# A gated mix of sliding-window attention and a SwiGLU block on one core: projections moved forward, one half-tile later, last operands scaled before the product

## The chip, the cores and the metric

The kernel runs on one core of one Trainium2 chip. The metric is the time of one execution on the device, in microseconds (us); lower is better. The core has five engines that run side by side and wait for one another through semaphores: TensorE (PE in the profile; its weight loads are PEld), VectorE (DVE), ScalarE (ACT), GpSimd (POOL) and SyncE (SP), whose queue issues most of the transfers.

## The reference

Two branches work on the same input `x` (2048 rows of 512) and are mixed row by row by a gate:

```python
def _A_ref(x, wqkv, wo):                       # attention
    B, S, D = x.shape
    H = 32; Dh = D // H; W = 256
    ... q, k, v of (x @ wqkv), 32 heads of 16
    scores = q @ k.T * Dh ** -0.5
    mask = (i - j >= 0) & (i - j < W)          # causal, the last 256 positions
    p = softmax(where(mask, scores, -1e9))
    return (p @ v) @ wo

def _B_ref(x, w_gate, w_up, w_down):           # F = 1792
    return (silu(x @ w_gate) * (x @ w_up)) @ w_down

g = sigmoid((x * gate_w).sum(-1, keepdims=True))
return g * _A_ref(...) + (1 - g) * _B_ref(...)
```

## The kernel before, in words

All products are formed from 32-bit operands split in two: a value is rounded to a high part (a cast on ScalarE), the rest is the low part (a subtraction on GpSimd or VectorE), and three matmuls (high by high, high by low, low by high) stand for one product. `split` at lines 64 to 70 does that; its cast is line 67, its subtraction line 70, whoever calls it.

The schedule is written out by hand: each engine runs its instructions in the order in which the program issues them, and so does each queue of transfers. The 32 heads are worked in 8 groups of 4; a block is 128 rows, a chunk (`c`) 512 rows, of which there are four, and a half (`hf`) two chunks.

**Start.** Nine matmuls on a tile of ones (18 in the trace, line 206) run while the input comes in; GpSimd fills the tile first (line 203), in the memory of a key tile. Then come, each as 12 whole matmuls from line 231 with a bank of PSUM as the target: the query and key projections `proj(g, c)` of groups 0 and 1, and V's blocks 0 to 3. `proj` ends with a copy out of PSUM on ScalarE (line 274) and a split; `stack(g, hf)` then moves a half's rows by twelve transfers on SP's queue (lines 284 and 285) into the tiles `QT` and `KT`, from which scores are formed.

**V's blocks.** V's blocks 4 to 15 follow in pairs on the two halves of the array's rows (`lanes`, line 251), pairs on `pb` and on `pa` by turns. Each pair takes two banks; ScalarE copies them out (line 442) and GpSimd sends them to `vd`. Woven in between are the 64 score matmuls of group 0 (`stage1`, line 301), each followed on VectorE by mask and row maximum (line 303); `put_max` (lines 314 to 319) writes a half's maxima into a row of `QT`. Behind V's blocks come, before the change, `proj(1, 2)`, `proj(1, 3)`, `stack(1, 1)` and the loads of V (`load_v`, line 330).

**Main loop.** 128 steps `t`, each of four sub-steps `hd`; four steps form a quad with the parts 0 to 3. In a sub-step PE does one score matmul of the next group (`stage1`), one transposed score matmul of this group (`stage2`, line 343, followed by the exponential on ScalarE, line 345, and selects on GpSimd, lines 347 and 350), and six lane matmuls of a projection or of the gate and up products (line 251; `unit` hands out four turns a quad: two on `pa`, two on `pb`). Once a quad the product with V is formed (`av`, line 367), and the generator `FIN` finishes the quad before: `finish` has five parts, a ScalarE copy (382), a VectorE addition out of PSUM (384), a transpose (388), reciprocal and multiplication (392, 393), and a transpose with a store (396, 397). Everything else is put into a table by step and sub-step with `later(t, hd, ...)` and runs when the loop gets there. In `group_half`, which takes up the projections of groups 2 to 7, each half has two splits, `half(0)` and `half(1)`, and then its `stack`. In the last 16 steps the scores of a next group are gone, and weights of the down projection are prepared instead (`early`, lines 653 and 657) with the row gate (637).

**The end.** The output projection and the down projection (a scheme of seven products of blocks, in the order of `ITEMS`) run as whole matmuls, three per product (`mm3`, lines 85 to 87); `halve` splits an operand, `JOBS` holds VectorE's work on finished banks, `DO` what is due at an item, and `scaled` multiplies a result by the gate (line 951), adds (953) and sends it (955). The last output tile is formed in two halves of 256 columns from the last three items; behind it VectorE multiplies by the gate (1072), adds the rest (1073) and SP sends it (1074).

Of the kernel before, what the change touches and what calls it, by code (L numbers as in the profile page):

```python
# [8 lines left out]
F32 = mybir.dt.float32  # L9
F32R = mybir.dt.float32r  # L10
AF = mybir.ActivationFunctionType
ALU = mybir.AluOpType
# [3 lines left out]
P = 128  # L16
S, D, H, DH, W, F = 2048, 512, 32, 16, 256, 1792
NK = D // P
NB = S // P
CH = 512  # L20
NCH = S // CH
# [14 lines left out]
def gated_mix(ctx, tc, xT, xn, w1a, w1b, wqk, wv, wo, wgu, wd, gw, outT):  # L36
# [4 lines left out]
    nc = tc.nc  # L41
# [16 lines left out]
    ring = ctx.enter_context(tc.tile_pool(name="ring", bufs=2))  # L58
# [32 lines left out]
    def run(gen, n=None):  # L91

        while n is None or n > 0:
            if next(gen, run) is run:
                break
            n = n and n - 1
# [5 lines left out]
    def slot(name, dtype=F32R):  # L102
        return stk.tile([P, S], dtype, name=name)
# [6 lines left out]
    KT = [[slot(f"k0{pr}") for pr in range(2)]]  # L110
# [82 lines left out]
    pp = ctx.enter_context(tc.tile_pool(name="pp", bufs=2, space=PSUM))  # L193
# [4 lines left out]
    with ExitStack() as A:  # L198
        sm = A.enter_context(tc.tile_pool(name="sm", bufs=2))


        ones = KT[0][0][:, :P].bitcast(F32)
        nc.gpsimd.memset(ones, 1.0)
        warm = pp.tile([P, CH], F32, name="pa")
        for _ in range(9):
            nc.tensor.matmul(warm[:, :P], ones, ones, start=True, stop=True)
# [13 lines left out]
        def x_pair(pool=None, name="x"):  # L220
            return tuple((pool or sm).tile([P, 2 * CH], F32R, name=f"{name}{w}", bufs=1) for w in ("hi", "lo"))
# [44 lines left out]
        def proj(g, c, pool, name):  # L266

            hf, cc = divmod(c, 2)
            if cc == 0:
                X[g, hf] = x_pair() if g == hf else x_pair(vpool, f"x{g}{hf}")  # L270

            def done(ps):
                raw = kept()
                nc.scalar.copy(raw, ps)
                split_qk(g, hf, cc, raw)
            todo = products(("p", g), c)
            return whole(pool, name, swapped(todo) if g == c == 0 else todo, done)

        def stack(g, hf):
            for pr in range(2):  # L280
                q, k = (halves_of(t[g % 2][pr])[hf] for t in (QT, KT))
                hi, lo = (x[32 * pr:] for x in X[g, hf])
                for b, (qx, kx) in enumerate(((hi, hi), (hi, lo), (lo, hi))):
                    nc.sync.dma_start(q[b::4].bitcast(F32), qx[:32].bitcast(F32))
                    nc.sync.dma_start(k[b::4].bitcast(F32), kx[64:96].bitcast(F32))
# [223 lines left out]
            run(proj(0, c, pp, "pa"))  # L509
        stack(0, 1)  # L510
        stack(1, 0)


        first = chain(*(stage1(0, b) for b in range(NB)))
# [12 lines left out]
                put_max(0, 0)  # L527
        run(first)
        put_max(0, 1)
        for c in range(2, NCH):  # L530
            run(proj(1, c, pp, "pb"))
        stack(1, 1)
        for n in range(4):
            load_v(n)
        vp.close()
# [6 lines left out]
        def later(t, hd, *fs):  # L542
            AT.setdefault((t, hd), []).extend(fs)
# [46 lines left out]
        def group_half(t, g, hf):  # L590

            t0 = t + 3 + hf

            def done(ps):
                places = [kept(), kept()]
                for m in range(2):
                    later(t0, 2 * m, lambda m=m: nc.scalar.copy(places[m], ps[m]))

                def half(m):
                    if m == 0:  # L600
                        X[g, hf] = x_pair()
                    split_qk(g, hf, m, places[m])
                first = t0 + (3 + g % 2) * hf
                later(first, 3, lambda: half(0))
                later(first + 1, 1, lambda: half(1))
                later(max(first + 1, (g - 1) * NB) if hf else first + 1, 3, lambda: stack(g, hf))
            return done

# [69 lines left out]
        for b in range(NB):  # L678
            t, hd = blocks[b]
            later(t, hd, lambda b=b: gate_block(b))  # L680
            if b > 1:
                t, hd = blocks[b - 2]
# [13 lines left out]
        FIN = iter(())  # L696
        for t in range(G * NB + 1):
            g, i = divmod(t, NB)
            d, part = divmod(t, NSLOT)
            if part == 0:  # L700
                turns = unit(t) if t < G * NB else [iter(())] * NSLOT
            s1 = stage1(g + 1, i) if t < g7 else iter(())
            s2 = stage2(g, i) if t < G * NB else iter(())
            for hd in range(4):
                run(s1, 1)
                if t < g7:
                    run(s2, 1)
                elif hd % 2 == 0:
                    run(s2, 2)
                run(turns[part], 3)  # L710
                for f in AT.pop((t, hd), ()):
                    f()
                if (part, hd) in ((0, 2), (1, 1), (1, 3), (2, 1)):
                    run(FIN, 1)
                if hd == 1 and part == 0:
                    if t:
                        ag, c = divmod(d - 1, NCH)
                        av(ag, c)
                        FIN = finish(ag, c)
                        run(FIN, 1)  # L720
            if i in (7, 15) and g + 1 < G:
                later(t + 1, 2, lambda g=g, i=i: put_max(g + 1, i // 8))
            if t >= 10 and t % 4 == 2 and t + 6 < G * NB:
                load_v((t + 6) // 4)
# [6 lines left out]
    with ExitStack() as B:  # L731
        got = B.enter_context(tc.tile_pool(name="got", bufs=10, side="right"))
        hp = B.enter_context(tc.tile_pool(name="hp", bufs=LEAD + 2, side="right"))
# [13 lines left out]
        def load_wo(k):  # L747
            raw = taken(wo[:, k])
            return lambda: split(woh[:, k], wol[:, k], raw, nc.scalar, nc.vector)
# [4 lines left out]
        PLACE = {}  # L754
# [30 lines left out]
        ITEMS = [("a", c, k) for c in range(NCH) for k in range(NK)]  # L785
# [4 lines left out]
        SRC, HALF, PARTS = {}, {}, {}  # L790
# [101 lines left out]
        GATE = {}  # L892
# [71 lines left out]
        def after(p, pr):  # L964

            two = bank(p, pr)
            for d in range(2):
                m = 2 * pr + d
                if p == 1:
                    JOBS.append(lambda d=d, m=m: nc.scalar.copy(saved(m), two[d]))  # L970
                if p == 5:
                    JOBS.append(lambda d=d, m=m: nc.scalar.copy(saved(4 + m), two[d]))
                if p == 6:
                    JOBS.append(lambda d=d, m=m: nc.vector.tensor_tensor(out=spare(m), in0=two[d], in1=saved(4 + m), op=ALU.subtract))
                if p == 2:
                    JOBS.append(lambda d=d, m=m: combined(2 * pr, d, two[d], saved(m), ALU.add))
                if p == 7:
                    JOBS.append(lambda d=d, m=m: combined(2 * pr + 1, 2 + d, two[d], saved(4 + m), ALU.subtract))
                if p == 3:
                    JOBS.append(lambda d=d, m=m: combined(2 * pr + 1, d, two[d], spare(m), ALU.add))  # L980
                if p == 4 and pr == 0:
                    JOBS.append(lambda d=d: scaled(2 * pr, 2 + d, column(), two[d]))

        late = [load_wo(k) for k in range(NK)]
        for e in ITEMS[:LEAD]:
            load(e)
# [21 lines left out]
        end = len(ITEMS) - 3  # L1008

        DO = {}  # L1010

        def on(n, f, *args):
            DO.setdefault(n, []).append(lambda: f(*args))

        for j in range(2 * NP):
            two = divmod(j, 2)
            n = WO + j
# [20 lines left out]
        for i in range(NP):  # L1038
            n = WO + 57 + 4 * (i // 2) + i % 2 - (i == 6)
            steps(n, (n + 6, n + 7), negated, NP + i)  # L1040
        for n, e in enumerate(ITEMS[:end]):
            if n + LEAD + AHEAD < WO:
                load(ITEMS[n + LEAD + AHEAD])
            for f in DO.pop(n, ()):
                f()
            while rows and at[(*rows[0], 0)] <= n + 6:
                load_sum(*rows.pop(0))
            if n + LEAD < len(ITEMS):
                halve(ITEMS[n + LEAD])
            if JOBS:  # L1050
                JOBS.pop(0)()
            if e[0] == "a":
                multiply_a(*e[1:])
                continue
            p, k, pr = e
            block(e)
            HALF.pop(e)
            if k == NP - 1:
                after(p, pr)
        while JOBS:  # L1060
            JOBS.pop(0)()
        two, t, part, rest = bank(4, 1), *(column() for _ in range(3))
# [4 lines left out]
        for cols in (slice(0, CH // 2), slice(CH // 2, CH)):  # L1067
            ps = pp.tile([P, CH], F32, name="pa")[:, cols]
            for n, (p, k, pr) in enumerate(ITEMS[end:]):
                hh, hl = HALF[p, k, pr]  # L1070
                mm3(ps, [(block_weights(p, k, 1), (hh[:, cols], hl[:, cols]))], start=n == 0, stop=n == 2)
            nc.vector.tensor_tensor(out=part[:, cols], in0=ps, in1=GATE[1][:, 2, cols], op=ALU.mult)
            nc.vector.tensor_tensor(out=part[:, cols], in0=part[:, cols], in1=rest[:, cols], op=ALU.add)
            nc.sync.dma_start(place(2, 3)[:, cols], part[:, cols])


# [34 lines left out]
```

## Time and profile before

| | |
|---|---|
| median of 3 runs | 801.77 us (801.17 to 802.3) |
| profiled execution | 801.55 us, of which the span from first to last instruction is 799.9 us |
| busy share of the span | PE 99%, PEld 87%, DVE 78%, ACT 54%, POOL 43% |
| mean HBM traffic | 119 GB/s |

Busy time of PE is no measure of speed by itself: matmuls overlap and their ends are modelled. What can be read exactly is the distance between the starts of two matmuls, and how far it is above what the same two take elsewhere in the trace.

### The profile page before, as it was taken

The page shows a single profiled execution, that of the slowest core. Times are in us where ns is not written, and L with a number is a line of the kernel's source. Part 1 is how long each engine was busy: PE and PEld are TensorE (multiplying, and loading weights), DVE is VectorE, ACT ScalarE, POOL GpSimd, SP SyncE. Part 2 cuts the span into 40 slices and gives each one's busy share as a digit, 9 for nine tenths or more (in the row PEclk, how much of TensorE's full clock was granted, in tenths as well). Part 3 has the DMA queues.
Part 4 walks back from the last instruction along what each step waited for, and adds up shares of the span by engine and source line. Part 5 has one row for each costly group of instructions (what it writes and reads, how often), then busy time and mean ns, then how long its engine had stood idle before and what let it go on. Part 6 is the DMA issues. An engine that isn't in the chain of part 4 may idle for free.

```text
span 799.9 us, 21441 instructions
## 1 busy us (share of the span) xinstructions
PE 794.2 (99%) x8247; PEld 698.2 (87%) x8247; DVE 626.2 (78%) x1689; ACT 432.6 (54%) x883; POOL 342.1 (43%) x643
## 2 busy tenths in 40 slices
PE   9999999999999999999999999999999999999998
PEld 8888999889889989899998998888988888888886
DVE  5397787878886887878776888888675478899896
ACT  7422556565565567555666656555643235554642
POOL 6712456565546556544656454546740111000112
PEclk9999999999999999999999999999999999999999
DMA  8574515425242453351533516425537898717435
GB/s 302 168 217 147 142 69 137 131 90 151 68 153 81 114 168 103 112 156 59 145 111 120 152 51 195 144 90 186 190 105 251 285 342 293 288 57 272 93 55 104
DMA packets 62107, 121.88 MB, mean 152 GB/s; under 512 B 10868, under 2 KB 19828, under 8 KB 61748
## 3 DMA queue, kind: packets, MB, share of 16 engines
q1 hardware_dynamic: 54756, 99.01, 40.1%
q0 software_dynamic: 7104, 21.24, 9.0%
q8 instruction: 65, 1.06, 0.6%
q14 instruction: 38, 0.31, 0.1%
q10 hardware_dynamic: 144, 0.26, 0.1%
HBM read 55.97 MB, written 39.34 MB: 119 GB/s over the span
## 4 chain that ended last, share of the span: by engine, by line
PE 98%; DVE 2%; issue 0%; POOL 0%; POOLq 0%
PE pa L251 24%; PE pb L251 24%; PE ps L301 7%; PE ps L343 5%; PE ps L367 5%; PE ps L87 4%; PE ps L86 4%; PE ps L85 4%; PE pb L367 4%; PE pa L231 2%; PE pb L231 2%; PE pa L87 2%; PE pb L86 2%; PE pa L86 2%; PE pb L87 2%; PE pb L85 2%
## 5 line engine op out<-in xcount | busy, mean ns | idle before, releaser
L303 DVE CUSTOM_DVE_ANT_0 ps<-ps,mask 128x384 f32<-128x384 f32 (+2 forms) x512 | 268.5, 540 | 99.4 <-PE ps L343 52.1
L345 ACT ACTIVATE pt<-ps 128x384 f32<-128x384 f32 (+2 forms) x512 | 238.0, 474 | 127.5 <-PE ps L343 68.0
L347 POOL TENSOR_SCALAR_AFFINE_SELECT pt<-pt 128x256 f32<-128x256 f32 x256 | 110.7, 433 | 197.4 <-ACT pt L345 195.5
L343 PE MATMUL ps<-q,k 64*128 64x384 f32 (+2 forms) x512 | 162.3, 335 | 0.0
L301 PE MATMUL ps<-k,q 63*128 63x384 f32 (+2 forms) x512 | 159.6, 332 | 0.5 <-DVE mx L303 0.5
L251 PE MATMUL pb<-xhi,wh 64*128 64x512 f32 x512 | 117.0, 396 | 0.0
L251 PE MATMUL pb<-xlo,wh 64*128 64x512 f32 x512 | 115.7, 391 | 0.0
L251 PE MATMUL pa<-xhi,wh 64*128 64x512 f32 x512 | 115.7, 394 | 0.0
L251 PE MATMUL pb<-xhi,wl 64*128 64x512 f32 x512 | 115.6, 391 | 0.0
L251 PE MATMUL pa<-xlo,wh 64*128 64x512 f32 x512 | 114.4, 392 | 0.0
L251 PE MATMUL pa<-xhi,wl 64*128 64x512 f32 x512 | 114.3, 391 | 0.0
L301 PEld LDWEIGHTS ps<-k,q 63*128 63x128 f32 x512 | 88.9, 185 | 13.4 <-DVE mx L303 3.3
L350 POOL TENSOR_SCALAR_AFFINE_SELECT pt<-pt 128x256 f32<-128x256 f32 x224 | 98.4, 439 | 0.0
L343 PEld LDWEIGHTS ps<-q,k 64*128 64x128 f32 x512 | 91.3, 185 | 5.2 <-issue 0.2
L303 DVE DVE_READ_ACCUMULATOR2_ANT mx<- 128x1 f32 x512 | 71.4, 139 | 0.0
L367 PE MATMUL ps<-pt,vg 64*32 64x320 f32 (+4 forms) x1408 | 70.6, 344 | 0.0
L367 PE MATMUL pb<-pt,vg 64*32 64x256 f32 (+3 forms) x1360 | 69.9, 349 | 0.0
L251 PEld LDWEIGHTS pb<-xhi,wh 64*128 64x128 f32 x512 | 63.1, 186 | 4.1 <-DVE o L384 0.3
L251 PEld LDWEIGHTS pb<-xhi,wl 64*128 64x128 f32 x512 | 62.6, 185 | 3.6
L251 PEld LDWEIGHTS pa<-xhi,wl 64*128 64x128 f32 x512 | 61.3, 185 | 3.9
L251 PEld LDWEIGHTS pb<-xlo,wh 64*128 64x128 f32 x512 | 62.6, 186 | 0.2
L251 PEld LDWEIGHTS pa<-xhi,wh 64*128 64x128 f32 x512 | 60.8, 186 | 1.9
(303 smaller groups left out, 1601.0 us busy)
## 6 DMA issues: line engine op xcount, KB each, us to landing
kept_h<-ev SPq DMA_DIRECT2D x52, 256.0 KB
od<-o POOLq DMA_DIRECT2D x32, 256.0 KB, 3.5
raw<-wgu SPq DMA_DIRECT2D x28, 256.0 KB
q<-xhi SPq DMA_DIRECT2D x56, 128.0 KB
k<-xhi SPq DMA_DIRECT2D x56, 128.0 KB
outT<-sg POOLq DMA_DIRECT2D x28, 256.0 KB, 4.0
vd<-vs POOLq DMA_DIRECT2D x8, 672.0 KB, 4.9
vg<-vd SPq DMA_DIRECT2D x32, 168.0 KB
```

What stands on the lines that cost most here:

```text
L85: nc.tensor.matmul(ps, lh, rh, start=start and i == 0, stop=False, skip_group_check=skip)
L86: nc.tensor.matmul(ps, lh, rl, start=False, stop=False, skip_group_check=skip)
L87: nc.tensor.matmul(ps, ll, rh, start=False, stop=stop and i == n - 1, skip_group_check=skip)
L231: nc.tensor.matmul(ps, w, x, start=n == 0, stop=n == len(todo) - 1)
L251: mm = nc.tensor.matmul(ps[me], w[r], x[r], start=not second and i == 0, stop=bool(second) and i == n - 1)
L301: nc.tensor.matmul(ps[:, :n], QT[g % 2][pr][r, q0:q0 + P], KT[g % 2][pr][r, k0:k0 + n], start=True, stop=True)
L303: mx = nc.vector.tensor_tensor_reduce(out=ps[:, :n], in0=ps[:, :n], in1=mask[:, 3 * P - n:], scale=1.0, scalar=NEG, op0=ALU.add, op1=ALU.m ...
L343: nc.tensor.matmul(ps[:, :n], KT[g % 2][pr][r, k0:k0 + P], QT[g % 2][pr][r, k0:k0 + n], start=True, stop=True)
L345: BEHIND.append(nc.scalar.activation(pt[:, j, :n], ps[:, :n], AF.Exp, scale=SCALE))
L347: nc.gpsimd.affine_select(out=pt[:, :, :P], in_=pt[:, :, :P], pattern=[[0, 2], [1, P]], compare_op=ALU.is_ge, fill=0.0, base=0, channel_mu ...
L350: nc.gpsimd.affine_select(out=pt[:, :, 2 * P:], in_=pt[:, :, 2 * P:], pattern=[[0, 2], [-1, P]], compare_op=ALU.is_ge, fill=0.0, base=-1, ...
L367: nc.tensor.matmul(AV[g, c][h][32 * j:32 * j + 32, q0 - c * CH:q1 - c * CH], VG[4 * g + kb // 4][o, kb % 4, 17 * j:17 * j + 32], PT[g, kb, ...
```

## The change

Four edits in one:

1. The warm-up matmuls read a constant that the program's preamble has filled, instead of a tile that GpSimd fills.
2. `proj(1, 2)`, `proj(1, 3)` and `stack(1, 1)` come ahead of V's blocks 4 to 15, directly behind `stack(1, 0)`; they stay on `pb`.
3. In `group_half`, `half(1)` of the second half (`hf` 1) of odd groups runs at sub-step 3 instead of 1; and in the main loop the parts of `FIN` that fall on a sub-step are issued ahead of what the table holds for it.
4. For the last tile the three operands are multiplied by the gate and split before the product (`SCALED`), issued behind the last item of the main list; behind the product only the addition is left.

```diff
-        ones = KT[0][0][:, :P].bitcast(F32)
-        nc.gpsimd.memset(ones, 1.0)
+        ones = nc.const_aps.tensor(1.0, [P, P], F32)
...
         stack(0, 1)
         stack(1, 0)
+        for c in range(2, NCH):
+            run(proj(1, c, pp, "pb"))
+        stack(1, 1)
...
         run(first)
         put_max(0, 1)
-        for c in range(2, NCH):
-            run(proj(1, c, pp, "pb"))
-        stack(1, 1)
         for n in range(4):
             load_v(n)
...
-                later(first + 1, 1, lambda: half(1))
+                later(first + 1, 3 if hf and g % 2 else 1, lambda: half(1))
...
                 run(turns[part], 3)
+                if (part, hd) in ((0, 2), (1, 1), (1, 3), (2, 1)):
+                    run(FIN, 1)
                 for f in AT.pop((t, hd), ()):
                     f()
-                if (part, hd) in ((0, 2), (1, 1), (1, 3), (2, 1)):
-                    run(FIN, 1)
...
+        SCALED = []
+
+        def scaled_halves(i):
+
+            e = ITEMS[end + i]
+            raw = PLACE["raw"][:, i]
+            nc.vector.tensor_tensor(out=raw, in0=PARTS["v", e[1], e[2]], in1=GATE[1][:, 2], op=ALU.mult)
+            SCALED.append([ring.tile([P, D], F32R, name=w) for w in ("wh", "wl")] if i < 2 else
+                          [hp.tile([P, CH], F32R, name=w) for w in ("hh", "hl")])
+            nc.scalar.copy(SCALED[i][0], raw)
+
+        def rest_of(i):
+            hi, lo = SCALED[i]
+            nc.vector.tensor_tensor(out=lo, in0=PLACE["raw"][:, i], in1=hi.bitcast(F32), op=ALU.subtract)
...
         end = len(ITEMS) - 3
         DO = {}
+        DO[end] = [lambda i=i, f=f: f(i) for f in (scaled_halves, rest_of) for i in range(3)]
...
+        for f in DO.pop(end):
+            f()
         while JOBS:
             JOBS.pop(0)()
...
             for n, (p, k, pr) in enumerate(ITEMS[end:]):
-                hh, hl = HALF[p, k, pr]
+                hh, hl = SCALED[n]
                 mm3(ps, [(block_weights(p, k, 1), (hh[:, cols], hl[:, cols]))], start=n == 0, stop=n == 2)
-            nc.vector.tensor_tensor(out=part[:, cols], in0=ps, in1=GATE[1][:, 2, cols], op=ALU.mult)
-            nc.vector.tensor_tensor(out=part[:, cols], in0=part[:, cols], in1=rest[:, cols], op=ALU.add)
+            nc.vector.tensor_tensor(out=part[:, cols], in0=ps, in1=rest[:, cols], op=ALU.add)
             nc.sync.dma_start(place(2, 3)[:, cols], part[:, cols])
```

## The prediction

> **What bounds the kernel now.** I read the page's engine shares first, then the waits of TensorE, then the timeline at each place that the diff touches (its rows: start, duration, engine, line, operation, out<-in, shapes, count; in brackets the idle time before and what ended it).
>
> ```profile
> PE 794.2 (99%) x8247; PEld 698.2 (87%) x8247; DVE 626.2 (78%) x1689; ACT 432.6 (54%) x883; POOL 342.1 (43%) x643
> PE pa L206 <- POOL k L203: 1.1, 1, 1.1
> PE ps L301 <- DVE mx L303: 0.5, 2, 0.2
> ```
>
> TensorE (PE) is busy in 99% of the span and is recorded as waiting three times, 1.6 us in all. So no edit can bring much, and an edit can only bring something where the distance between matmul starts is longer than the matmul needs: at the two ends, at those two waits, and where the order of matmuls changes kind. The profiled execution took 801.55 us for a span of 799.9 us; the median of the runs is 801.77 us, 0.22 us above it. I work each term out on the profiled execution and read the sum on both.
>
> **Warm-up on a constant.**
>
> ```profile
> 0.81 0.39 SPq L410 DMA_DIRECT2D raw<-w1a  x1
> 1.14 4.21 PE L206 MATMUL pa<-k 128*128 128x128 f32 x18 [1.14 <-POOL k L203]
> 4.06 0.62 ACT L67 CAST xhi<-q 128x512 fp32r<-128x512 f32 x1
> 4.94 0.33 PEld L231 LDWEIGHTS pa<-xhi,wh 128*128 128x128 f32 x1
> 6.38 0.56 DVE L70 TENSOR_TENSOR wl<-raw,wh 128x384 fp32r<-128x384 f32 x1
> 6.43 0.63 PE L231 MATMUL pa<-xhi,wh 128*128 128x512 f32 x1
> 6.86 0.58 PE L231 MATMUL pa<-xlo,wh 128*128 128x512 f32 x1
> 7.51 0.40 PE L231 MATMUL pa<-xhi,wh 128*128 128x512 f32 x1
> 7.74 0.39 PE L231 MATMUL pa<-xhi,wl 128*128 128x512 f32 x1
> ```
>
> PE waits for GpSimd's fill of `ones`. Other queues start at 0.81, so the 18 warm-up matmuls can begin some 0.3 earlier and end at about 4.65 instead of 4.95. The first real weight load stands at 4.94, but its input is ready at 4.06 + 0.62 = 4.68: it gains 0.2 to 0.25. The matmuls behind it start 0.43 apart (6.43, 6.86) until about 7.3 and 0.23 apart afterwards (7.51, 7.74): the array is slow at first, and what is gained in the slow stretch is worth about half in the fast one (0.1), plus 0.1 if the fast stretch also comes a little earlier. I take -0.2; ends 0 and -0.7 (a rival below).
>
> **Second group's projections ahead of V's blocks.** The same 24 matmuls of `proj(1, 2)` and `proj(1, 3)` run earlier. What changes is who stands next to whom.
>
> ```profile
> 33.15 0.39 PE L231 MATMUL pa<-xhi,wl 128*128 128x512 f32 x1
> 33.47 0.50 PE L251 MATMUL pb<-wvh,xhi 64*128 64x512 f32 x2
> 72.05 0.34 PE L301 MATMUL ps<-k,q 63*128 63x384 f32 x2
> 72.65 0.40 PE L231 MATMUL pb<-xlo,wh 128*128 128x512 f32 x1
> 77.68 0.39 PE L231 MATMUL pb<-xhi,wl 128*128 128x512 f32 x1
> 78.00 0.44 PE L343 MATMUL ps<-q,k 64*128 64x384 f32 x1
> 78.17 0.50 PE L251 MATMUL pa<-xhi,wh 64*128 64x512 f32 x2
> 72.30 1.08 ACT L442 COPY vs<-pa 128x512 f32<-128x512 f32 x2 [2.23 <-issue]
> 78.11 0.59 ACT L274 COPY ev<-pb 128x512 f32<-128x512 f32 x1 [1.44 <-PE pb L231]
> ```
>
> *Lost.* Each of `pa` and `pb` has two buffers, and a lane pair takes both. Before, the V blocks' first pair (`pb`, 33.47) followed projections on `pa`, and the main loop's first pair (`pa`, 78.17) followed projections on `pb`: the buffers had been emptied. After, both follow work on their own name. (a) `proj(1, 3)` ends on `pb`; by the rows at 77.68 and 78.11, ScalarE's copy begins 0.43 after the last matmul's start and takes 0.59. So the second lane starts 1.02 after that matmul at the earliest, instead of 0.32 (33.15 to 33.47): +0.70. (b) The last V pair ends on `pa`; its two copies run 72.30 to 73.38, so on that scale the main loop's second lane starts at 73.38. Undisturbed it would start at 72.39, two score steps of 0.17 (78.00 to 78.17) after 72.05: +0.99.
>
> *Won.* Before, PE changes from lanes to whole matmuls and back. From 72.05 to 72.65 is 0.60 where 0.40 is due (0.17 for the pair of scores, 0.23 for one matmul), and from 77.68 to 78.17 is 0.49 where 0.40 is due: -0.3.
>
> The edit comes to 0.70 + 0.99 - 0.3 = +1.4 us. The ends: -0.3 if both copies are hidden, +2.6 if a cast of ScalarE (0.62) stands ahead of each copy. I take +1.4: the rows give both copies their start directly behind their matmuls.
>
> [...]
>
> The twelve transfers of `stack(1, 1)` and their waits move on SP's queue from behind to ahead of the weight prefetch and the first `put_max`; GpSimd's two subtractions for them (1.3 us each) move ahead of V's stores. Later in V's stretch nothing on PE waits for either queue, and in the main loop SP is relieved. I cost it at nothing; what it costs if late is a rival.
>
> **Odd groups' low half.** Both waits of PE for VectorE (DVE) are of this kind (the two rows without an operation come from the chain of work that ended last, the one with three durations, in ns, from the answer on its line):
>
> ```profile
> 199.42 1.28 POOL L70 TENSOR_TENSOR xlo<-ev,xhi 128x512 fp32r<-128x512 f32 x1
> 199.83 1.15 DVE o L393
> 330.68 1.15 DVE o L393
> L393 DVE TENSOR_TENSOR o<-o,rc x32: 424/486/1154, 101.6 to 600.1; 128x256 f32<-128x256 f32 x32
> 200.46 0.41 PE L251 MATMUL pa<-xhi,wh 64*128 64x512 f32 x2
> 201.79 0.45 PE L251 MATMUL pa<-xhi,wh 64*128 64x512 f32 x2
> 462.21 0.42 PE L251 MATMUL pa<-xhi,wh 64*128 64x512 f32 x2
> 463.02 0.50 PE L251 MATMUL pa<-xhi,wh 64*128 64x512 f32 x2
> ```
>
> `finish` multiplies by the reciprocal (L393): 0.49 us at the median, 1.15 at 199.83 and 330.68, the two on the chain. The first lies under GpSimd's 1.28 us subtraction, the low half of group 3's second projection; 330.68 is the same step of group 5. The masks behind it on DVE come late, a score bank is not free, and one step of PE takes 1.33 (200.46 to 201.79) where group 7, with less DVE work before it, takes 0.81 (462.21 to 463.02): 0.52, twice. Half 1 now comes two steps, some 1.75 us, later; its cast waits behind the step's exponentials and its subtraction behind their selects, when L393 is done. GpSimd has room (43%). Change: -1.04; ends 0 and -1.1.
>
> The reordering of `finish` against the other steps matters only where both use DVE: L384 goes ahead of `put_max` and of the four late quads' casts:
>
> ```profile
> 546.28 0.69 DVE L637 SCALAR_TENSOR_TENSOR xhi<-xlo,xhi 128x512 f32<-128x512 f32 x1 [1.51 <-DMA xlo<-xn]
> ```
>
> The casts, which ran while PE formed the products that L384 needs, now wait until L384 ends, and all DVE steps of the quad behind them too, by an estimated 2 us; DVE's idle 1.51 at 546.28, in the first of these quads, takes most of that up, and no wait of PE is listed there. I take 0, ends -0.2 and +0.5.
>
> **Scaled operands at the end.**
>
> ```profile
> 784.95 0.69 DVE L951 TENSOR_TENSOR sg<-sg,xlo 128x512 f32<-128x512 f32 x1
> 785.56 0.69 DVE L70 TENSOR_TENSOR hl<-got,hh 128x512 fp32r<-128x512 f32 x1
> 788.28 0.69 DVE L70 TENSOR_TENSOR hl<-xlo,hh 128x512 fp32r<-128x512 f32 x1
> 791.70 0.69 DVE L951 TENSOR_TENSOR sg<-ps,xlo 128x512 f32<-128x512 f32 x1 [2.73 <-PE ps L87]
> 795.89 0.42 DVE L1072 TENSOR_TENSOR sg<-pa,xlo 128x256 f32<-128x256 f32 x1
> 796.35 0.43 DVE L1073 TENSOR_TENSOR sg<-sg 128x256 f32<-128x256 f32 x1
> ```
>
> Behind the last matmul stand a multiplication and an addition; the multiplication goes: 796.35 - 795.89 = -0.46. The price is three multiplications, three ScalarE copies and three subtractions, put behind the last split (788.28) and ahead of L951. DVE is idle there for 2.73 us. Six operations at 0.61 a start (784.95 to 785.56) end the block at 792.55, so L951 begins 0.85 late; the four steps from it, at up to 0.69 each, end at 795.31, and the first half's addition (0.42) at 795.73, before the last matmul's result at 795.89. So less than 0.2 us of cover is left. The scaled operands are there at 792.6; PE needs them 2.4 us before the end of its work (18 matmuls of half width), at about 793.5. I take -0.46; ends -0.5 and 0.
>
> **Sum.** -0.2 + 1.4 - 1.04 - 0.46 = -0.3: 801.25 against the profiled 801.55, and 801.5 on the median.
>
> **Rivals.**
> 1. *The copies are hidden* and the move is worth -0.3 instead of +1.4: 799.8. For it: no row of before shows PE waiting for a ScalarE copy of `pa` or `pb`. Against it: two buffers, both taken. Chance 0.13.
> 2. *The fast stretch opens at once.* PE starts earlier and may be fast from the first real matmul. The matmul at 7.74 needs the weights that DVE finishes at 6.38 + 0.56 = 6.94, so at most 0.7 is won, 0.5 more than I took: 801.0. For it: nothing in the rows says what sets 7.3. Chance 0.1. [...]
> 3. *SP's queue is late (slower).* Before, SP's last transfer of `stack(1, 0)`, then `put_max`:
>
> ```profile
> 45.54 0.54 SPq L284 DMA_DIRECT2D q<-x10hi  x1
> 57.31 0.60 SPq L285 DMA_DIRECT2D k<-x10hi  x1
> 66.07 1.03 SPq L319 DMA_DIRECT2D q<-md  x2
> ```
>
> Twelve transfers took 12.4 us, so `stack(1, 1)` would end at about 70.3 and both transfers of the maxima, which began 8.2 us after that before (57.9 to 66.07) because DVE was not ready, would be out 4 us after it and land by about 77, where the main loop needs them at 79.4 (78.0 + 1.4). It decides from some 2.5 us of lateness on: at 1.5 us a transfer instead of 1.03 the twelve end 5.6 later and the loop waits 3: 804.6. Chance 0.05.
> 4. *The odd half only moves its collision* to another DVE step: +1.04, 802.5.
>
> ```profile
> L388 DVE STREAM_TRANSPOSE o<-o 128x512 f32<-128x512 f32 x32 | 22.6, 705 | 0.0
> ```
>
>    Against it: the next step of `finish` there is a transpose, and all 32 of L388's kind average 0.705, so none is drawn out as L393 is. Chance 0.08.
>
> **Numbers.** The forecast has 0.64 and stands at 801.4 (the sum's two readings are 801.25 and 801.5), with a range of its own from 800.6 to 802.3. Rival 1's 799.8 and rival 4's 802.5 set the whole range, 799.6 to 802.7. A difference of 0.2%, 1.6 us, is what a measurement of this kernel can tell from none. Faster than 800.2: most of rival 1 and a tail, 0.17. Slower than 803.4: rival 3 and a tail, 0.06. Within: 0.77.
>
> **What would show it.** First warm-up matmul near 0.8 us. A new wait of PE for L274's and for L442's copies at the start of V's blocks and of the main loop, 0.7 to 1.1 us each. No L393 over 0.8 us, and no PE wait for L303 near 200 and 331 us. The last result's transfer one DVE step behind the last matmul. It is wrong if those copies are hidden, if SP holds `put_max`, or if the six added DVE steps reach past the last matmul.

## The result: 0.9% slower, lost at the start of the main loop and in one late quad

The changed kernel takes 808.96 us (median of 6 runs, 807.27 to 810.31) where the kernel before takes 801.53 (6 runs, 800.83 to 802.3): a ratio of 1.0093, 95% interval 1.0083 to 1.0103. Its profiled execution took 810.3 us for a span of 808.6, 8.7 us more than the 799.9 of before, and is among its longer ones. Line numbers of the changed kernel are one lower than those of before from the warm-up to the end's first lines (the exponential is line 344, was 345; the product with V 366, was 367; the last addition is 1089).

The engine shares and the clock row of the changed kernel's page, and behind them the waits of TensorE (us in total, times, the longest):

```profile
PE 797.7 (99%) x8247; PEld 694.1 (86%) x8247; DVE 628.5 (78%) x1693; ACT 434.5 (54%) x886; POOL 339.9 (42%) x642
PEclk9999899999999999999999999999999999999999
```

```profile
PE ps L342 <- ACT pt L344: 5.6, 2, 4.2
PE pa L205 <- PEq L1119: 0.8, 1, 0.8
PE ps L342 <- DVE mx L302: 0.6, 1, 0.6
PE pb L250 <- ACT ev L273: 0.2, 1, 0.2
```

PE's share is still 99%. What is new stands in the first row of the waits: two for the exponential, 5.6 us together, which before did not have at all. The second row is the start of the warm-up matmuls at 0.85; the third comes where the main loop begins (78.61) and was not there before either. The clock row has one slice below full, the fifth (81 to 101 us). The first V product of the main loop, in before and then in the changed kernel, and the last one, give a ruler:

```profile
93.84 0.42 PE L367 MATMUL pb<-pt,vg 64*32 64x256 f32 x4
594.55 0.31 PE L367 MATMUL ps<-pt,vg 64*32 64x128 f32 x4
```

```profile
78.61 0.95 PE L250 MATMUL pa<-xhi,wh 64*128 64x512 f32 x2
101.42 0.42 PE L366 MATMUL pb<-pt,vg 64*32 64x256 f32 x4
603.74 0.31 PE L366 MATMUL ps<-pt,vg 64*32 64x128 f32 x4
```

| stretch | before | after | difference |
|---|---|---|---|
| to the main loop's first lane matmul (78.17, 78.61) | 78.17 | 78.61 | +0.44 |
| from there to the first product with V | 15.67 | 22.81 | +7.14 |
| to the last product with V | 500.71 | 502.32 | +1.61 |
| to the end of the span | 205.30 | 204.86 | -0.44 |

The four add up to 8.75. The second row is one wait and what follows it; the timeline and the table of stretches (length, busy time by engine, granted clock, DMA share, GB/s) of the changed kernel:

```profile
77.94 1.08 ACT L441 COPY vs<-pa 128x512 f32<-128x512 f32 x2 [2.22 <-issue]
79.06 0.18 PEld L250 LDWEIGHTS pa<-xhi,wh 64*128 64x128 f32 x1 [0.27 <-ACT vs L441]
79.30 0.89 POOL L444 DMA_DIRECT2D vd<-vs  x1 [2.41 <-ACT vs L441]
79.56 0.57 SPq L316 DMA_DIRECT2D md<-mtt  x1
84.42 0.98 SPq L318 DMA_DIRECT2D q<-md  x2
84.49 0.49 ACT L344 ACTIVATE pt<-ps 128x384 f32<-128x384 f32 x1 [5.48 <-DMA md<-mtt]
85.04 0.69 PE L342 MATMUL ps<-q,k 64*128 64x384 f32 x1 [4.20 <-ACT pt L344]
```

```profile
82.00:84.00 2.00, 0.00 (x0) 0.00 (x0) 0.00 (x0) 0.00 (x0) 0.00 (x0) 0.88 0.52 159
84.00:90.40 6.40, 5.36 (x28) 5.37 (x30) 0.90 (x5) 2.77 (x7) 2.76 (x5) 0.50 0.50 151
```

From 82 to 84 us no engine does anything. ScalarE waits 5.48 us with the main loop's first exponential, PE has no free score bank and waits 4.20, and then runs at half clock until 90.4. From the matmul that waited (85.04; in before its counterpart stands at 79.79) to the first product with V are 16.38 against 14.05, so the stretch at half clock costs 2.3. The remaining 0.6 of the 7.14 lie ahead of the wait, where the second lane is late (79.06). The transfer that the profile names as the one waited for, `md<-mtt` (the row maxima), is not the only candidate: GpSimd's last store of V blocks, `vd<-vs`, went out 0.26 before it, and this store takes 4.9 us to land, the median of its kind in before too. 79.30 + 4.9 = 84.2, which is 0.3 ahead of the exponential. In before the same store and the same exponential stand like this (behind them a row of the page's list of transfers: count, KB each, median us to landing):

```profile
73.67 0.89 POOL L445 DMA_DIRECT2D vd<-vs  x1 [2.42 <-ACT vs L442]
79.25 0.48 ACT L345 ACTIVATE pt<-ps 128x384 f32<-128x384 f32 x1
79.79 0.44 PE L343 MATMUL ps<-q,k 64*128 64x384 f32 x1
```

```profile
vd<-vs POOLq DMA_DIRECT2D x8, 672.0 KB, 4.9
```

73.67 + 4.9 = 78.6, before the exponential is due at 79.25. Why an exponential should wait for a store of V is in the code, where the main loop begins:

```python
vp.close()
ptp = A.enter_context(tc.tile_pool(name="ptp", bufs=13, side="right"))
```

`vpool` held the tiles `vs` from which V is stored; `ptp`, which holds the exponentials' results, is opened on the same side, in the memory that `vpool` gives back. Then the first writer into it would have to wait for all that still reads the old tiles; the experiments below test that. In before `proj(1, 2)` and `proj(1, 3)` lay between the store and that writer; the change moved them away.

The third row of the ruler has gains and one loss. Distances between successive V products: the two odd quads of the prediction (steps 28 to 31 and 60 to 63) went from 16.71 and 16.72 to 16.19 and 16.18; several others from 16.54 to 16.63 down to 16.44 to 16.46; and the quads of steps 112 to 115 and 116 to 119 went from 15.66 and 14.95 up to 17.67 and 16.48, +3.5. The timeline there, of before and then of the changed kernel, with one stretch of the latter behind it:

```profile
539.43 0.58 SPq L317 DMA_DIRECT2D md<-mtt  x1
543.85 0.91 SPq L587 DMA_DIRECT2D kept_h<-ev  x2
548.01 0.60 ACT L567 ACTIVATE ev<-pa 128x512 f32<-128x512 f32 x1 [0.24 <-DMA kept_h<-ev]
```

```profile
544.28 0.69 DVE L383 TENSOR_TENSOR o<-pb,o 128x512 f32<-128x512 f32 x1 [1.37 <-ACT o L381]
544.89 0.96 DVE L652 CAST q<-ev 128x512 fp32r<-128x512 f32 x2
546.42 0.59 SPq L316 DMA_DIRECT2D md<-mtt  x1
550.86 0.91 SPq L586 DMA_DIRECT2D kept_h<-ev  x2
555.26 0.60 ACT L566 ACTIVATE ev<-pa 128x512 f32<-128x512 f32 x1 [2.25 <-DMA kept_h<-ev]
556.29 0.82 PE L342 MATMUL ps<-q,k 64*128 64x384 f32 x2 [1.41 <-ACT pt L344]
```

```profile
558.00:561.50 3.50, 3.50 (x57) 2.14 (x61) 1.76 (x4) 0.00 (x0) 0.67 (x2) 0.52 0.08 29
```

`FIN`'s addition (L383) now stands ahead of the casts and of `put_max` on DVE, and waits 1.37 for ScalarE. So `put_max`'s transfer leaves 1.4 us later, counted from the quad's first V product (541.1 to 546.42 against 535.5 to 539.43), SP's queue behind it too, and with it the store `kept_h<-ev`, which frees a buffer that the gate's tanh needs. The tanh waits 2.25 instead of 0.24, the exponentials behind it on ScalarE are late, PE waits 1.41, and a stretch at half clock follows (last row, clock 0.52).

### The profile page after: what moved, and what is told of

Same layout as the page of the kernel before. It is cut to its first block, busy times and chain, and to the rows that moved or that the text cites. A ratio compares the mean times of both kernels' runs of the same rounds, so it can differ in the third digit from the quotient of the medians.

```text
span 808.6 us, 21440 instructions
## 1 busy us (share of the span) xinstructions
PE 797.7 (99%) x8247; PEld 694.1 (86%) x8247; DVE 628.5 (78%) x1693; ACT 434.5 (54%) x886; POOL 339.9 (42%) x642
## 3 DMA queue, kind: packets, MB, share of 16 engines
q8 instruction: 65, 1.06, 0.5%
## 4 chain that ended last, share of the span: by engine, by line
PE 87%; issue 1%; DVE 1%; DMA 1%; ACT 0%; SPq 0%; ACTq 0%
PE pb L250 22%; PE pa L250 22%; PE ps L300 6%; PE ps L366 5%; PE ps L342 5%; PE ps L85 4%; PE ps L86 4%; PE ps L87 4%; PE pb L366 4%; PE pa L85 2%; PE pa L86 2%; PE pa L87 2%; PE pb L85 2%; PE pb L86 2%; PE pb L87 2%; PE pa L775 1%
## 5 line engine op out<-in xcount | busy, mean ns | idle before, releaser
L300 PE MATMUL ps<-k,q 63*128 63x384 f32 (+2 forms) x512 | 167.0, 331 | 0.0
L250 PE MATMUL pb<-xhi,wh 64*128 64x512 f32 x512 | 112.6, 395 | 0.0
L250 PE MATMUL pb<-xhi,wl 64*128 64x512 f32 x512 | 111.1, 393 | 0.0
L250 PE MATMUL pb<-xlo,wh 64*128 64x512 f32 x512 | 111.0, 392 | 0.0
L300 PEld LDWEIGHTS ps<-k,q 63*128 63x128 f32 x512 | 94.8, 185 | 15.4 <-DVE mx L302 2.1
L366 PE MATMUL ps<-pt,vg 64*32 64x320 f32 (+4 forms) x1408 | 71.8, 348 | 0.0
L250 PEld LDWEIGHTS pa<-xhi,wl 64*128 64x128 f32 x512 | 58.5, 185 | 5.3
L250 PEld LDWEIGHTS pb<-xhi,wh 64*128 64x128 f32 x512 | 57.9, 186 | 5.2
L250 PEld LDWEIGHTS pb<-xhi,wl 64*128 64x128 f32 x512 | 57.8, 185 | 5.1
L250 PEld LDWEIGHTS pa<-xhi,wh 64*128 64x128 f32 x512 | 58.1, 187 | 3.4 <-ACT vs L441 0.3
L250 PEld LDWEIGHTS pa<-xlo,wh 64*128 64x128 f32 x512 | 58.9, 186 | 0.2
```

The source lines that it names most:

```text
L250: mm = nc.tensor.matmul(ps[me], w[r], x[r], start=not second and i == 0, stop=bool(second) and i == n - 1)
L300: nc.tensor.matmul(ps[:, :n], QT[g % 2][pr][r, q0:q0 + P], KT[g % 2][pr][r, k0:k0 + n], start=True, stop=True)
L366: nc.tensor.matmul(AV[g, c][h][32 * j:32 * j + 32, q0 - c * CH:q1 - c * CH], VG[4 * g + kb // 4][o, kb % 4, 17 * j:17 * j + 32], PT[g, kb, ...
```

## Experiments

Theory: the two losses are (1) the wait for V's last store through reused memory, uncovered by the move, and (2) the late buffer that `FIN`'s new place brings in steps 112 to 127. Rivals: for (1) the transfer of the maxima, as the profile names it, or SP's queue; for (2) ScalarE or DVE simply having too much work there. Each kernel is timed against the kernel before on the same chip. Edits are against the changed kernel where nothing else is said.

### The move and the late order, undone one by one

Move undone (only its times are used; its one profiled execution, with a span of 2020.7 us, is left aside, so that its late quads were not seen):

```diff
         stack(1, 0)
-        for c in range(2, NCH):
-            run(proj(1, c, pp, "pb"))
-        stack(1, 1)
...
         put_max(0, 1)
+        for c in range(2, NCH):
+            run(proj(1, c, pp, "pb"))
+        stack(1, 1)
```

> The changed kernel with proj(1, 2), proj(1, 3) and stack(1, 1) put back behind V's blocks; the other edits stay. Theory: the wait of TensorE for the main loop's first exponentials (4.2 us) and the stretch at half clock behind it come from the move alone, the wait near 554 us from issuing FIN ahead of the table; so 801.5 of before - 0.5 (start) - 1.5 (odd groups and the quads behind put_max) + 3.5 (wait near 550 us and its half clock) - 0.5 (end) = 802.5 us, and the two last long quads (17.67, 16.48) stay. Rival: the wait near 550 us is only a consequence of the delay at the start; then 799.0 us.

Late order undone, `FIN` behind the table from step 112 on:

```diff
-                if (part, hd) in ((0, 2), (1, 1), (1, 3), (2, 1)):
+                if t < g7 and (part, hd) in ((0, 2), (1, 1), (1, 3), (2, 1)):
                     run(FIN, 1)
                 for f in AT.pop((t, hd), ()):
                     f()
+                if t >= g7 and (part, hd) in ((0, 2), (1, 1), (1, 3), (2, 1)):
+                    run(FIN, 1)
```

> The changed kernel with FIN behind the table again in the last 16 steps only (t >= 112). Theory: there L384 ahead of put_max and the casts delays VectorE, SP's queue behind it and with it the store of kept_h whose buffer the next tanh takes; with the old order the quads of 17.67 and 16.48 return to 15.7 and 15.0: 809.0 - 3.5 = 805.5 us. Rival: the wait there comes from another edit: 809 us.

Both undone:

> The changed kernel with proj(1, 2), proj(1, 3), stack(1, 1) back behind V's blocks and FIN behind the table again in the last 16 steps. If the losses are those two alone: 801.6 of before - 0.5 (start) - 1.04 (two odd quads) - 0.5 (FIN ahead of put_max in the quads before) - 0.49 (end) = 799.1 us, no wait of TensorE for an exponential over 0.5 us, full clock from about 5 us on. Rival: part of the gains came from the later phase of the changed kernel; then 800.0 to 800.9, as with the projections alone put back.

| | `FIN` first throughout | `FIN` behind the table from step 112 |
|---|---|---|
| projections moved | 808.96, ratio 1.0093 [1.0083, 1.0103] | 806.74, 1.0063 [1.0048, 1.0078] |
| not moved | 800.87, 0.9992 [0.9982, 1.0002] | 799.12, 0.9971 [0.996, 0.9982] |

The move costs 1.0% in the first column and 0.9% in the second (7.6 us), the late order 0.3% and 0.2%. The two losses are separate and nearly additive, and together they are the whole loss: with both undone the rest of the change gains 0.29%. With the late order undone the two late quads take 16.11 and 14.96, while PE's wait at the main loop's start stays at 4.0; with both undone PE waits for no exponential at all. Only the third time came out as expected (799.1). The theories for the first two said 802.5 and 805.5, because they put the late order at the 3.5 of the one profiled execution; in the medians it costs 2.2 with the projections moved and 1.8 without.

### What the main loop's first exponential waits for

Rival: the transfer of the maxima. The second `put_max` is moved from the start to step 2, so that no transfer of maxima stands ahead of the exponential:

```diff
-        put_max(0, 1)
...
+        later(2, 2, lambda: put_max(0, 1))
```

> The changed kernel with the second put_max of group 0 taken out from ahead of the main loop and issued at step 2 of it, so that SP's md transfer, which the profile names as what ended ScalarE's wait of 5.48 us, does not exist yet. Theory: the first exponential still starts at about 84.4, when V's last store has landed; TensorE waits 4.0 to 4.2 us, the profile now names another transfer, 807 to 809 us. Rival: the md transfer was the cause; TensorE waits under 1 us, 802 to 803 us.

Measured 808.11, ratio 1.0078 [1.0064, 1.0092]. Timeline:

```profile
79.62 0.89 POOL L444 DMA_DIRECT2D vd<-vs  x1 [2.41 <-ACT vs L441]
84.17 0.49 ACT L344 ACTIVATE pt<-ps 128x384 f32<-128x384 f32 x1 [4.85 <-issue]
84.72 0.44 PE L342 MATMUL ps<-q,k 64*128 64x384 f32 x1 [3.58 <-ACT pt L344]
```

The transfer of the maxima is gone from the place and the wait is not: the rival falls. The profile now names no releaser ("issue"). The store lands 4.3 us after its issue here, at 83.9, and 4.9 in the changed kernel, at 84.2; in both the exponential starts 0.3 behind the landing. The chain of work of the changed kernel agrees (start, us, what): the queue of ScalarE moves again here, ahead of `q<-md` at 84.42, which waits for the maxima.

```profile
84.26 0.04 ACTq L344
```

The store itself. The tile `vs1`, stored last, is given a pool of its own, `osb` (a tile needed later) is laid over that one, and `ptp` goes to the other side:

```diff
+        vp1 = ExitStack()
+        last = vp1.enter_context(tc.tile_pool(name="vlast", bufs=1, side="right"))
         vp = ExitStack()
...
-        vs = [vpool.tile([P, G, 2, VW], F32, name=f"vs{i}") for i in range(2)]
+        vs = [(last if i else vpool).tile([P, G, 2, VW], F32, name=f"vs{i}") for i in range(2)]
...
         vp.close()
-        ptp = A.enter_context(tc.tile_pool(name="ptp", bufs=13, side="right"))
-        osb = A.enter_context(tc.tile_pool(name="osb", bufs=1))
+        vp1.close()
+        osb = A.enter_context(tc.tile_pool(name="osb", bufs=1, side="right"))
+        ptp = A.enter_context(tc.tile_pool(name="ptp", bufs=13))
```

> The changed kernel with the V tile of the last two blocks (vs1) in a pool of its own, whose memory is later taken by osb and not by the tiles of the exponentials (pt). Theory: the first exponential waits until every transfer that reads the pool that pt replaces has landed, V's last store (issued 79.3, landed about 84.3) last; without that one it waits for the store before it (issued 76.0), so it starts at about 81, TensorE waits under 1 us instead of 4.2, the clock stays up: 809.0 - 3.4 - 2.9 = 802.7 us. Rival: SP's transfers of the second maxima (md, landed 84.4), which the profile names as the releaser, hold it: 809 us, exponential at 84.5.

Measured 804.0, ratio 1.0025 [1.0015, 1.0035], some 5 us less than the changed kernel. Timeline, and one row of the chain of work that ended last (start, us, what):

```profile
76.72 0.89 POOL L446 DMA_DIRECT2D vd<-vs  x1 [8.82 <-ACT vs L443]
80.02 0.89 POOL L446 DMA_DIRECT2D vd<-vs  x1 [2.41 <-ACT vs L443]
81.43 0.49 ACT L344 ACTIVATE pt<-ps 128x384 f32<-128x384 f32 x1 [1.70 <-PE ps L300]
81.97 0.44 PE L342 MATMUL ps<-q,k 64*128 64x384 f32 x1 [0.42 <-ACT pt L344]
```

```profile
76.72 3.00 DMA vd<-vs
```

The exponential runs 1.4 us after the last store was issued, and this store lands 4.5 us after its issue, so the exponential does not wait for it any more; PE's wait is 0.42, and the granted clock stays at 1.00 (82 to 90.4). This shows loss (1). The chain now names the store before the last, issued at 76.72 from the tile that stayed in `vpool`: it lands 4.5 us later, at 81.2, again just ahead of the exponential. The theory's 802.7 was 1.3 too low. The kernel stays slower than before because its first V product still comes 2.2 us later (96.01 against 93.84), because the late quad keeps its loss (17.15), and because of a 0.8 us wait of PE for DVE near the end that came with the moved pools and whose cause stays open.

### What the late quad waits for

The order stays as changed, but the two stores `kept_h` due in step 113 are issued five sub-steps earlier, in step 112, so that the buffer comes free earlier; no engine has less to do:

```diff
-                    later(t + 5, 2, lambda m=m: nc.sync.dma_start(kept_h[f, 2 * hf + m], hs[m]))
+                    later(*((t + 4, 1) if t == g7 - 4 else (t + 5, 2)), lambda m=m: nc.sync.dma_start(kept_h[f, 2 * hf + m], hs[m]))
```

> The changed kernel, FIN first everywhere, but in the quad at t = 112 the two kept_h stores are issued five sub-steps earlier, ahead of put_max and the gate's fetches on SP's queue. Theory: the tanh there waits for the store's buffer alone; it finds it free, TensorE does not wait and the clock stays up: 805.5 us. Rival: VectorE's own lateness (casts and products 1.4 us later) holds TensorE: the wait stays, 808 to 809 us.

Measured 806.75, ratio 1.0063 [1.0048, 1.0078]: the same as with the late order undone (806.74), and 1.2 above the theory, which again took off 3.5. The store and the tanhs that waited for it:

```profile
540.58 0.92 SPq L586 DMA_DIRECT2D kept_h<-ev  x2
551.67 0.60 ACT L566 ACTIVATE ev<-pa 128x512 f32<-128x512 f32 x1 [0.59 <-PE pa L250]
552.91 0.62 ACT L566 ACTIVATE ev<-pa 128x512 f32<-128x512 f32 x1
```

No tanh waits for the store now, and the two quads take 15.72 and 14.97. So it was the buffer, not the amount of work. The same with the move undone as well:

> The changed kernel with the projections back behind V's blocks, FIN ahead of the table everywhere, and the two kept_h stores of the quad at t = 112 issued five sub-steps earlier. Theory: with the store out of the way FIN first costs nothing there: quads 27 and 28 at 15.7 and 15.0, 799.1 us as with the old order. Rival: FIN first still costs in the last quads: 799.5 to 800.9 us.

Measured 799.1, ratio 0.9968 [0.9956, 0.998]: with the kernel that has both undone (799.12) the fastest of this study, and faster than both kernels.

`FIN` first as the only edit of the kernel before:

```diff
+                if (part, hd) in ((0, 2), (1, 1), (1, 3), (2, 1)):
+                    run(FIN, 1)
                 for f in AT.pop((t, hd), ()):
                     f()
-                if (part, hd) in ((0, 2), (1, 1), (1, 3), (2, 1)):
-                    run(FIN, 1)
```

> The kernel before with FIN ahead of the table, nothing else. Theory: the quads at 16.62 and 16.54 before become 16.46 (ten of them, -0.1 to -0.16 each, together about -1), the quad at t = 112 grows by 1.5 without a fall of the clock and by 3.5 with one; L393 under GpSimd's subtraction stays at 1.15 us. 801.5 to 802.2 us, in some executions 3 us more. Rival: the order of FIN changes nothing: 801.7 us with all quads as before.

Measured 802.34, ratio 1.0008 [0.9999, 1.0016], just above the range of the theory. Its trace has both sides:

```profile
548.19 0.60 ACT L567 ACTIVATE ev<-pa 128x512 f32<-128x512 f32 x1 [2.13 <-DMA kept_h<-ev]
549.23 0.82 PE L343 MATMUL ps<-q,k 64*128 64x384 f32 x2 [1.27 <-ACT pt L345]
```

The late quad takes 17.17 (+1.5). The quads at 16.62 and 16.54 to 16.57 come down to 16.46 or 16.47, and the two odd quads stay at 16.72 and 16.70. From the first V product to the last it is 501.41 against 500.71: +0.7, so the other quads gain 0.8.

### The wait for a bank

`proj(1, 2)` and `proj(1, 3)` go to `pa` instead of `pb`, with the late order undone, to be held against 806.74:

```diff
-            run(proj(1, c, pp, "pb"))
+            run(proj(1, c, pp, "pa"))
```

> The changed kernel with proj(1, 2) and proj(1, 3) on pa instead of pb, and FIN behind the table in the last 16 steps (806.74 us without the change of banks). Theory: V's first pair on pb finds its banks empty; its second lane starts 0.3 behind the last projection matmul instead of 1.07, the stretch from there to V's last matmul takes 38.4 instead of 39.1, 806.0 us. Rival: the pairs on pa behind it wait instead, 806.7 us.

Measured 806.22, ratio 1.0057 [1.0044, 1.0071]. V's blocks now start without the wait:

```profile
39.42 0.50 PE L250 MATMUL pb<-wvh,xhi 64*128 64x512 f32 x2
85.33 0.68 PE L342 MATMUL ps<-q,k 64*128 64x384 f32 x1 [4.17 <-ACT pt L344]
```

Both lanes start together, and from there to the last V matmul it is 38.36, as in before (33.47 to 71.83), where the changed kernel takes 39.08 (38.39 to 77.47). The wait is there and is worth 0.72 in the trace; 0.5 us in the medians, which their intervals do not separate from nothing.

### The other parts alone, on the kernel before

The warm-up on a constant:

```diff
-        ones = KT[0][0][:, :P].bitcast(F32)
-        nc.gpsimd.memset(ones, 1.0)
+        ones = nc.const_aps.tensor(1.0, [P, P], F32)
```

> The kernel before with the warm-up matmuls on the constant, nothing else. Theory: they start at 0.85 instead of 1.14, the first real weight load at 4.70 instead of 4.94, and V's first block at 11.1 to 11.9 instead of 11.6, by where the clock rises (5.0, 4.9, 4.2 and 3.75 us in four traces, 7.24 before): -0.3 to -0.5, 801.2 us. Rival: only the start of the warm-up moves and the inputs set the rest: 801.6 us.

Measured 801.38, ratio 1.0003 [0.9993, 1.0013]. The first real matmul starts at 4.68 instead of 5.00, and V's first block at 11.61, in before at 11.62: what was won at the start was gone by the time of V. Nor is the 4.68 shown to come from the edit: the kernel with the odd half alone (below) begins its warm-up at 1.14 and its first real matmul at 4.68 too.

The scaled operands at the end (`scaled_halves`, `rest_of`, `SCALED` and the shorter last step, as in the change):

> The kernel before with the scaled operands of the last tile, nothing else. Theory: one VectorE step less behind the last matmul and the nine added operations inside its idle time: -0.45 to -0.5, 801.15 us. Rival: the added steps push the last addition: 801.6 us or more.

Measured 801.07, ratio 0.9993 [0.9984, 1.0002]. From the last matmul's start to the end of the span it is 3.83 instead of 4.28: -0.45 in the trace, 0.6 in the medians, not separated from nothing there.

The odd groups' low half:

```diff
-                later(first + 1, 1, lambda: half(1))
+                later(first + 1, 3 if hf and g % 2 else 1, lambda: half(1))
```

> The kernel before with half(1) of odd groups' second half at sub-step 3, nothing else (FIN behind the table as before). Theory: two quads lose 0.52 each because L393 no longer runs under GpSimd's subtraction: 800.6 us, both L393 under 0.6 us, and the quads of 16.62 (third to last of each odd group) stay, as they go with FIN ahead of put_max. Rival: the gain needs FIN ahead of the table: 801.6 us.

Measured 800.36, ratio 0.9983 [0.9974, 0.9992]. The multiplications of `finish` (count, then ns least/median/most, as in the prediction's row):

```profile
L393 DVE TENSOR_TENSOR o<-o,rc x32: 424/474/569, 101.7 to 599.0; 128x256 f32<-128x256 f32 x32
```

The two of 1.15 us are gone, and the two odd quads take 16.22 and 16.23 instead of 16.71 and 16.72.

## Why the prediction was wrong, and where it was right

**The step that failed most** is the last one on the move: "The twelve transfers of `stack(1, 1)` ... GpSimd's two subtractions for them ... move ahead of V's stores. Later in V's stretch nothing on PE waits for either queue ... I cost it at nothing". I followed what moves, and whom it would meet at its new place. I did not ask what the moved work had been hiding at its old place. That was 5.7 us of PE between V's last blocks and the main loop, and behind it ran the last copy, GpSimd's store and 4.9 us of landing. The rows were there: 73.67 plus 4.9 against 79.25 leaves 0.7 us of cover. Without the 5.7 the main loop is about 5 us short, and 4.2 of it is PE's wait. The same 5.7 us had let VectorE catch up with its masks, which end at 73.6 in before; without them PE waits 0.58 for one at 78.61, which was no term either. What was missing beside the rows is that `ptp` is laid over `vpool`: the exponential and the store share no name. The half clock after the wait, 2.3 us in the profiled execution, was not among my terms. Where the sum had +1.4 for the whole edit, the move cost 7.6 (806.74 against 799.12).

**The second** is `FIN`: "DVE's idle 1.51 at 546.28 ... takes most of that up, and no wait of PE is listed there. I take 0, ends -0.2 and +0.5". It was wrong on both sides. The delay on DVE was 1.4 rather than the estimated 2, but DVE's idle time did not help, because the delay left DVE at once through `put_max` into SP's queue and reached ScalarE through a buffer, where before already waited 0.24 (548.01) and so had no slack. The late quad lost 1.5 and, in the profiled execution of the changed kernel, 3.5 with the half clock. The -0.2 was also too small: on the other quads the new order gains about 0.8.

**Rival 3** had the right sign with the wrong mechanism. SP's queue was not late, since taking its transfer of the maxima away left the wait; the queue that mattered was GpSimd's, and not for its length but for the landing of its last store.

**Right, by their own steps:** (a) the second lane of V's blocks, forecast 0.70 late:

```profile
38.50 0.59 ACT L273 COPY ev<-pb 128x512 f32<-128x512 f32 x1 [1.43 <-PE pb L230]
39.13 0.49 PE L250 MATMUL pb<-wvh,xhi 64*128 64x512 f32 x1 [0.25 <-ACT ev L273]
```

The copy starts 0.43 after the last projection's start (38.07) and PE's second lane directly behind it: 39.13 against 38.39, and 0.72 over the stretch. So the copies are not hidden, and rival 1 falls. (b) The main loop's second lane starts at 79.06, right behind the two copies from 77.94 (1.08), 1.6 us after the last V matmul's start at 77.47; forecast was 73.38 - 71.8 = 1.6. I read it as costing nothing of its own in the changed kernel, since PE stood still behind it anyway. With the last V tile apart, where PE's wait is 0.42, the stretch from the main loop's first lane (79.33) to the first product with V is 16.69 against 15.67, so that some 0.6 are left for it. (c) The odd half: -1.04 forecast, -1.06 in the changed kernel, -0.98 alone; rival 4 falls. (d) The end: -0.46 forecast, -0.45 alone. The row that ends it has the room that I put at under 0.2:

```profile
804.34 0.42 DVE L1089 TENSOR_TENSOR sg<-pa,sg 128x256 f32<-128x256 f32 x1
805.08 0.42 DVE L1089 TENSOR_TENSOR sg<-pa,sg 128x256 f32<-128x256 f32 x1 [0.32 <-PE pa L87]
```

DVE waits 0.32 for the last matmul, so the six added steps did not reach it. The warm-up's -0.2 stays open: the warm-up matmuls start at 0.85 as said, and the end of the span shows none of the gain; the interval, -0.6 to +1.0 us, does not exclude the -0.2. Rival 2 stays open with it, because the time of full clock varies by more than the 0.3 that the edit moves (4.02 to 7.24 us, last section).

The other terms add up. The forecast's -0.2 - 1.04 - 0.46 and `FIN`'s -0.8 on the other quads make -2.5; the kernel with both losses undone measured -2.6. Of these the -0.2 is a forecast and not a measurement. The move's 7.6 and the late order's 2.2 are differences of the measured kernels themselves, so their sum with the -2.6, +7.2 against a measured +7.4, is no test of its own.

## What to carry to other kernels

Before work is moved away, list what was issued ahead of it and lands behind it: it was that work's cover. Here the first exponential inherited the wait for V's last store, through reused memory, and PE stood 4.20 us; so see also which tile pool is opened where one was closed, and which store reads the old tiles last. Where two steps of one engine change places, follow each to its transfers, the queue behind these and the buffers that they free, to the engine that waits there; idle time of the first engine does not settle it, as DVE's 1.51 us did not here. Of a bundle of edits, each was worth its own kernel: here small gains of 2.6 us together were hidden under two losses of 10.

## What the runs showed of the hardware that I had not expected

**A wait of 4.2 us cost 6.5.** After PE's wait at the main loop's start the granted clock fell to half: for 6.83 us in the changed kernel and in the one with `pa` (waits of 4.20 and 4.17, mean clock 0.993 and 0.995), for 3.41 us with the late order undone, with the early store and with the later `put_max` (waits of 4.00, 4.24 and 3.58, mean clock 0.998 in each). The half clock began while PE still stood (83.53, PE back at 85.04), so the 2.3 lost behind the wait came from the other 5.3 us at half clock. How much half clock follows differs between executions of one kernel: of the changed kernel's six, two have a mean clock of 0.993 (810.3), three 0.996 (808.61 to 809.19) and one 0.998 (807.27). In its profiled execution the clock fell once more in the late quad, for 3.41 us from 557.98, behind the wait of 1.41 at 556.29. Waits of 1.3 us there (with `vs1` apart, and with the later `put_max`) and of 1.27 (`FIN` first as the only edit) were followed by no half clock. The length of the wait alone does not give that of the half clock, since 4.24 was followed by 3.41 and 4.17 by 6.83; what else decides was not shown.

**The releaser named is one of several.** At 84.49 the profile named `md<-mtt`, issued 0.26 after the store that was the cause and landing at about the same time (`q<-md`, which needs it, goes out at 84.42). With that transfer gone it named nothing at all, and only with the last tile apart did the chain name a `vd` store. Where an engine waits for several transfers at once, the name is a candidate to be tried.

**The clock's rise at the start wanders.** By the first record of full clock in each trace (the profile's stretches give 1.00 from the start), it came to full at 7.24 us in before, and at 5.43, 5.29, 4.02 and 5.67 in the four kernels with one part alone, of which only the first has the earlier warm-up; 0.3 us of an earlier start cannot be seen against that.
